# A kernel of attention and two expert layers: in the second layer, the next expert's rows are fetched ahead of the output so far

## The chip, the cores and the metric

The program runs on one core of a Trainium2 chip. The metric is the device time of one execution in microseconds (us), as the median of several runs. TensorE (PE in the rows, PEld for its weight loads), VectorE (DVE), ScalarE (ACT), GpSimd (POOL) and SyncE (SP) each run their own list of instructions in order, and wait for each other by semaphores. SP issues the transfers of weights on one DMA queue, POOL issues the indirect transfers (rows picked by a list of row numbers) on another; both queues share 16 DMA engines.

## The reference, cut to what matters

Attention makes a table of 1152 tokens with 512 numbers each. A first layer sends each token to one of 8 experts. The second layer, on its result `x`, sends each token to its two best experts and adds up what they give:

```python
out = np.zeros((N, D), dtype=np.float32)
for e in range(E):
    for k in range(2):
        mask = top2[:, k] == e
        if not mask.any():
            continue
        h = np.maximum(x[mask] @ w1[e], 0.0)
        out[mask] += top2_w[mask, k, None] * (h @ w2[e])
return out.astype(np.float32)
```

Here N is 1152, D is 512, E is 8, and the hidden width of an expert is 1024.

## The kernel before

The kernel first does the attention, then the eight experts of the first layer, then the eight of the second. Only the loop over the experts 1 to 7 of the second layer is touched (lines 1775 to 1783 before); one pass of it is called an expert here.

An expert takes up to 288 tokens in the straight path: two blocks of 128 rows, and a third block of 32 rows that is only computed if the expert has more than 256 tokens. That third block is `rest(e)`, behind a branch at line 1780. Every number is kept as a sum of two reduced-precision parts, so weights are split into a high part by ACT (line 167) and a low part by DVE (line 170) after SP has fetched them, and every product is three matmuls (lines 198 to 200).

For an expert the work is this:

- `prev` (line 1577), twice: POOL fetches the rows of the output so far for each block into `pv` (shown as `px` in rows, since these tiles were named so earlier). The output holds what the experts before have added, so this waits until the previous expert's rows have landed in memory.
- `next_rows` and `rows2` (line 1418, in `gather`): POOL fetches the rows of `x` for the next expert's two blocks into `g0` and `g1`, and for this expert's third block into `g2`. These read `x_d`, which the first layer has finished.
- `blocks`: PE makes the hidden layer (matmuls to `h`, operands `xh`, `xl`), ACT and DVE turn it into `hh` and `hl` (lines 1145 and 1148), and PE makes the output (matmuls to `y`).
- `prep`: in the midst of the `y` matmuls PE turns the fetched rows by transposes (line 1015), ACT and DVE make `xh` and `xl` of them (lines 1018 and 1021), which the next expert's first matmul reads. The third block's rows go the same way into `xp`.
- `to_out`: DVE scales `y` and adds the old rows of the output (line 1583), and POOL writes the rows back (line 1586, `out_dram<-o`).

The order on each engine is set when the program is built. `F.add` enters an operation with its engine ("P", "A", "V", "G" for PE, ACT, DVE, GpSimd), a cost and what it depends on; `F.run` is a small planner that picks, for each engine, which entry comes next; `after=` is the earliest planned time of an entry. On the chip each engine takes its list in that order whatever the planner thought of times. SP issues a load of the weight chunk that comes seven later whenever a chunk has been split.

Of the kernel before, what the change touches and what calls it, by code (L numbers as in the profile page):

```python
# [41 lines left out]
def _off(ap):  # L42
    return bass.IndirectOffsetOnAxis(ap=ap, axis=0)
# [3 lines left out]
def attention_moe_moe2(ctx, tc, q, k, v, wg1, w1a, w2a, cap, wg2, wn2, noise, w1b, w2b, out):  # L47
    nc = tc.nc
    B, H, S, D = q.shape
    E, DM, F = w1a.shape  # L50
# [67 lines left out]
    def whole(u):  # L118
        return u < 8 * E and u % 8 >= 8 - WHOLE
# [55 lines left out]
    def w1_at(e, kk, f0, f1):  # L175
        s = slot(8 * e + kk)
        return whi[s][:, f0:f1], wlo[s][:, f0:f1]
# [19 lines left out]
    def mm3(o, sh, sl, mh, ml, first, last):  # L197
        nc.tensor.matmul(o, sh, mh, start=first, stop=False)  # L198
        nc.tensor.matmul(o, sh, ml, start=False, stop=False)  # L199
        nc.tensor.matmul(o, sl, mh, start=False, stop=last)  # L200

    xT = [(wa.tile([128, KD, 256 + R], F32R, name=f"xh{i}"), wa.tile([128, KD, 256 + R], F32R, name=f"xl{i}")) for i in range(1)]
# [913 lines left out]
    def blocks(F, e, x, more, finish, deps=(), done={}, apart=False):  # L1116

        xh, xl = x
        hh, hl = hT
        hp = {}  # L1120
        lo = []
        rows = 256 + more
        per = 1 if more else 2

        def l1(f, bank=None):
            if bank is not None:
                hp[f // per] = bank
            o = hp[f // per][:, (f % per) * rows:(f % per) * rows + rows]
            for kk in range(KD):
                sh, sl = w1_at(e, kk, f * 128, f * 128 + 128)  # L1130
                mm3(o, sh, sl, xh[:, kk, :rows], xl[:, kk, :rows], kk == 0, kk == KD - 1)

        def part(t, g):
            return t[:, per * g:per * g + per, :rows]

        def of(g):
            return hp[g][:, 0:per * rows].rearrange("p (f n) -> p f n", f=per)

        def plain(g):
            w = [whole(8 * e + 4 + (per * g + i) // 2) for i in range(per)]  # L1140
            assert w[0] == w[-1]
            return w[0]

        def relu(g):
            nc.scalar.activation(part(hfull[0], g - (KF - 2 * WHOLE) // per) if plain(g) else part(hh, g), of(g), AF.Relu)  # L1145

        def low(g):
            nc.vector.scalar_tensor_tensor(part(hl, g), of(g), 0.0, part(hh, g).bitcast(F32), op0=OP.max, op1=OP.subtract)  # L1148

        p = None  # L1150
        w1 = [done.get(8 * e + kk) for kk in range(KD)]
        for g in range(KF // per):
            c = 1.62 if more else 1.44
            first = p = F.add("P", c, lambda b, g=g: l1(per * g, b), [p] + list(deps) + w1, take="h")
            for i in range(1, per):
                p = F.add("P", c, lambda g=g, i=i: l1(per * g + i), [p])
            if g == KF // per - 1:
                for kk in range(KD):
                    if 8 * e + kk in F.hold:
                        F.hold[8 * e + kk]["deps"].append(p)  # L1160
            a = F.add("A", 0.41 if more else 0.6, lambda g=g: relu(g), [p], frees=first if plain(g) else None)
            lo += [a if plain(g) else F.add("V", 0.46 if more else 0.69, lambda g=g: low(g), [a], frees=first)] * per
        a = product2(F, e, 0, finish, [p, *lo], done)
        return [a, product2(F, e, 1, finish, [ends.pop() if apart else p, *lo], done)]
# [3 lines left out]
    def product2(F, e, blk, finish, lo=None, done={}):  # L1168

        hp = {}  # L1170
        n = 128 if blk < 2 else R

        def l2(f, bank=None):
            if f == 0:
                hp["y"] = bank[:n]
            product(hp["y"], e, f, slice(blk * 128, blk * 128 + n), f == 0, f == KF - 1)

        p, *lo = lo or [None] * (KF + 1)
        for f in range(KF):
            d = [p, lo[f], done.get(8 * e + 4 + f // 2)]  # L1180
            if f == 0:
                p = first = F.add("P", takes(e, f), lambda b: l2(0, b), d, take="y")
            else:
                p = F.add("P", takes(e, f), lambda f=f: l2(f), d)
        ends[:] = [p]
        return finish(lambda: hp["y"], blk, p, first)

    def splits(F, us):

        done = {}  # L1190
        for u in us:
            a = F.add("A", 0.95, lambda u=u: split(u, 0), [done.get(order[turn[u] - RAWS - MORE])], needs=u)
            F.hold[over(u)] = a
            if u % 8 in BESIDE:
                done[u] = F.add("G", 1.9, lambda u=u: split(u, 3), [a], loads=behind(u), tail=F.par["split"])
                continue
            b = F.add("V", 0.6, lambda u=u: split(u, 1), [a])
            done[u] = F.add("V", 0.6, lambda u=u: split(u, 2), [a, b], loads=behind(u), tail=F.par["split"])
        return done
# [185 lines left out]
    def count(t, e):  # L1385
        return nc.values_load(t[0:1, e:e + 1], min_val=0, max_val=NT, skip_runtime_bounds_check_because="a count of tokens")
# [17 lines left out]
    G = {}  # L1404
# [68 lines left out]
    for e in range(E):  # L1473
        for u in range(8 * e + EARLY, 8 * e + 8) if e else ():
            load(u)
        if e + 1 == E:
            F = Flow()
# [3 lines left out]
        def beside(F, first):  # L1481
            done = splits(F, units(e))
            nxt = post(F, first, last=True)[0] if first is not None else None
            if e + 1 < E:
                for blk, n in BLK:
                    d = F.add("G", 1.04, lambda blk=blk, n=n: row1(e + 1, blk, n)) if e else None
                    prep(F, lambda blk=blk: xr[e + 1, blk], n, xT[(e + 1) % 2], 128 * blk, deps=[d], when=(WHEN0 if e == 0 else F.par["when"]) + 1.5 * blk)
            else:
                d, _ = rows2(F, (0, 0), 0, 0, tis[0])
                prep(F, lambda: G[0, 0][2], 128, xT[0], 0, deps=[d])  # L1490
            return done, nxt
# [47 lines left out]
        with cmp.Else():  # L1539
            F = Flow(SMALL if e else FIRST)  # L1540
            begin(F)
            done, nxt = beside(F, last)
# [23 lines left out]
    def apart(ins, key):  # L1566

        if own["e"] != key[0]:
            own["e"], own["ins"] = key[0], []
        for o in own["ins"]:  # L1570
            tc.declare_no_dep(ins.ins, o.ins, reason="other rows")
        own["ins"].append(ins)
# [3 lines left out]
    def prev(ti, i, n=128):  # L1576
        ins = nc.gpsimd.indirect_dma_start(out=pv[i][:n], out_offset=None, in_=out, in_offset=_off(ti[:n, 0:1]),  # L1577
                                           bounds_check=NT - 1, oob_is_err=False)

    def to_out(F, y, key, i, p, first, n=128, deps=()):  # L1580
        def go():
            o = G[key, "o"] = os_[i]
            nc.vector.scalar_tensor_tensor(o[:n], y(), G[key][0][:n], pv[i][:n], op0=OP.mult, op1=OP.add)  # L1583

        def send():
            ins = nc.gpsimd.indirect_dma_start(out=out, out_offset=_off(G[key][1][:n, 0:1]), in_=G[key, "o"][:n], in_offset=None,  # L1586
                                               bounds_check=NT - 1, oob_is_err=False)
            if key[1] != "more":
                apart(ins, key)

        a = F.add("V", 0.66, go, [p, F.outs.get(i)] + list(deps), frees=first)
        F.outs[i] = F.add("G", 1.04, send, [a])
# [9 lines left out]
    def arm(e):  # L1602
        F = Flow(SECOND)
        if e + 1 < E:
            F.add("P", 0.3, lambda: many.update(n=count(cnt2, e)), after=10.0)
        done = splits(F, units(E + e))
        next_rows(F, e)
        if e + 1 == E:
            F.add("G", 0.2, lambda: nc.gpsimd.drain(), after=6.0)  # L1609
        else:  # L1610
            d, _ = rows2(F, (e, 2), e, 2, n=R)
            prep(F, lambda: G[e, 2][2], R, pair, 0, deps=[d], when=F.par["when"] + 4)
        blocks(F, E + e, xT[e % 2], 0, lambda y, blk, p, first: to_out(F, y, (e, blk), blk, p, first), done=done, apart=e + 1 == E)
        F.close(F.run())

    def rest(e):
# [123 lines left out]
    F = Flow(KNOWN)  # L1740
    done = splits(F, units(E))
# [31 lines left out]
    state["u"] = min(NU, 8 * E + SLOTS)  # L1773
    came, later = later, ({}, {})
    for e in range(1, E):
        for blk in range(2):
            prev(G[e, blk][1], blk)
        arm(e)
        if e + 1 < E:
            with tc.If(many["n"] > 256):  # L1780
                rest(e)
        state["u"] = min(NU, 8 * (E + e) + SLOTS)
        came, later = later, ({}, {})
# [32 lines left out]
```

## Time and profile before

| | |
|---|---|
| median of 3 runs (lowest, highest) | 559.38 us (557.72, 559.82) |
| the profiled execution's own time | 557.14 us |
| its span in the trace | 555.5 us |
| PE busy | 517.0 us, 93% of the span |
| DVE, ACT, POOL busy | 378.9, 294.1, 138.4 us |

The span runs from the first to the last instruction of the trace, and the execution's own time holds 1.64 us more around it. The rest of the trace is read by stage: the shares over the whole span mix attention and both layers.

### The profile page before, as it was taken

The numbers are of one execution on the slowest core, as the hardware profiler recorded it, in microseconds if no ns is written. First come the engines' busy times: TensorE is split into PE (matmuls) and PEld (weight loads), VectorE is DVE, ScalarE is ACT, GpSimd is POOL, SyncE is SP. The second block draws the span as 40 slices with busy tenths as digits, with TensorE's granted clock in tenths as the row PEclk, the third lists the DMA queues.
The fourth block names the chain that finished last, engine by engine and source line by source line (L and its number), as shares of the span: only waits on it lengthen the run. The fifth ranks groups of instructions, "written<-read, shape, count | busy, mean of one in ns | idle before, by whom it ended". The sixth has DMA issues, their size and how long they took to land. (4 is left out here: it accounts for less than half of the span.)

```text
span 555.5 us, 10106 instructions
## 1 busy us (share of the span) xinstructions
PE 517.0 (93%) x3381; PEld 422.8 (76%) x3381; DVE 378.9 (68%) x1008; ACT 294.1 (53%) x580; POOL 138.4 (25%) x225
## 2 busy tenths in 40 slices
PE   3999999999869999999999999989999999969996
PEld 3778777878647776787976967888989886949794
DVE  7899988888548988757674678464848562917441
ACT  5888878871347687544533536252635442716130
POOL 3000000000462234405233133142513132514131
PEclk9999999999999999999999999999999999979999
DMA  6998896423458878754632442638658591545220
GB/s 136 221 240 229 220 230 188 123 77 109 137 176 290 265 240 296 232 189 138 206 133 64 170 137 71 226 125 284 221 205 280 188 327 48 187 180 165 86 66 35
DMA packets 71176, 99.17 MB, mean 179 GB/s; under 512 B 37130, under 2 KB 40586, under 8 KB 71088
## 3 DMA queue, kind: packets, MB, share of 16 engines
q1 hardware_dynamic: 63600, 83.16, 47.6%
q0 software_dynamic: 6432, 14.71, 8.4%
q8 instruction: 39, 0.64, 0.5%
q14 instruction: 49, 0.40, 0.2%
q10 hardware_dynamic: 1056, 0.26, 0.2%
HBM read 87.53 MB, written 12.25 MB: 180 GB/s over the span
## 5 line engine op out<-in xcount | busy, mean ns | idle before, releaser
L170 DVE TENSOR_TENSOR wl<-raw,wh 128x512 fp32r<-128x512 f32 x140 | 91.6, 685 | 12.0 <-ACT wh L167 11.6
L167 ACT ACTIVATE wh<-raw 128x1024 fp32r<-128x1024 f32 x70 | 71.1, 1052 | 20.1 <-PEq L1780 12.5
L170 DVE TENSOR_TENSOR both<-raw,both 128x512 fp32r<-128x512 f32 x100 | 66.0, 684 | 8.9 <-ACT both L167 8.4
L167 ACT ACTIVATE both<-raw 128x1024 fp32r<-128x1024 f32 x50 | 51.3, 1054 | 10.0 <-PEq L1780 8.3
L198 PE MATMUL h<-xh,wh 128*128 128x256 f32 (+1 forms) x184 | 52.9, 287 | 0.5
L199 PE MATMUL h<-xl,wh 128*128 128x256 f32 (+1 forms) x184 | 52.6, 286 | 0.0
L200 PE MATMUL h<-xh,wl 128*128 128x256 f32 (+1 forms) x184 | 52.5, 285 | 0.0
L1018 ACT ACTIVATE xh<-tp 128x512 fp32r<-128x512 f32 (+1 forms) x37 | 19.0, 536 | 59.0 <-PE tp L1015 57.3
L1021 DVE TENSOR_TENSOR xl<-tp,xh 128x512 fp32r<-128x512 f32 (+1 forms) x37 | 21.9, 610 | 35.3 <-ACT xh L1018 35.1
L1145 ACT ACTIVATE hh<-h 128x512 fp32r<-128x512 f32 (+1 forms) x46 | 24.1, 523 | 38.7 <-PE h L200 32.3
L1586 POOL DMA_INDIRECT out_dram<-o,T2i x16 | 18.5, 1156 | 96.9 <-DVE o L1583 94.8
L1148 DVE SCALAR_TENSOR_TENSOR hl<-h,hh 128x512 fp32r<-128x512 f32 (+1 forms) x46 | 27.5, 597 | 22.1 <-ACT hh L1145 18.0
L198 PE MATMUL h<-xh,both 128*128 128x256 f32 (+1 forms) x136 | 39.2, 288 | 2.7 <-DVE hl L1148 1.4
L199 PE MATMUL h<-xl,both 128*128 128x256 f32 (+1 forms) x136 | 39.0, 287 | 0.0
L200 PE MATMUL h<-xh,both 128*128 128x256 f32 (+1 forms) x136 | 38.8, 285 | 0.0
L198 PE MATMUL y<-wh,hh 128*128 128x512 f32 (+1 forms) x94 | 38.3, 407 | 0.0
L200 PE MATMUL y<-wh,hl 128*128 128x512 f32 (+1 forms) x94 | 37.1, 394 | 0.0
L199 PE MATMUL y<-wl,hh 128*128 128x512 f32 (+1 forms) x94 | 36.9, 393 | 0.0
L550 ACT ACTIVATE pt<-s,negmax 128x128 f32<-128x128 f32 (+3 forms) x64 | 33.4, 526 | 6.4 <-DVE negmax L537 5.1
L526 PE MATMUL s<-both 128*128 128x256 f32 (+2 forms) x128 | 33.1, 371 | 3.8 <-ACT both L468 2.5
L198 PEld LDWEIGHTS h<-xh,wh 128*128 128x128 f32 x184 | 34.7, 189 | 2.1 <-issue 1.6
L199 PEld LDWEIGHTS h<-xl,wh 128*128 128x128 f32 x184 | 34.6, 188 | 0.0
(295 smaller groups left out, 1297.9 us busy)
## 6 DMA issues: line engine op xcount, KB each, us to landing
raw<-in_moe_w_dram SPq DMA_DIRECT2D x120, 512.0 KB, 5.1
wf<-in_moe_w_dram SPq DMA_DIRECT2D x8, 512.0 KB, 5.8
out_dram<-zero SPq DMA_DIRECT2D x3, 768.0 KB, 5.5
both<-both SPq DMA_DIRECT2D x14, 160.0 KB, 2.6
raw<-in_q_dram SPq DMA_DIRECT2D x16, 128.0 KB, 4.2
vn<-in_v_dram SPq DMA_DIRECT2D x16, 128.0 KB, 2.6
both<-both SPq DMA_DIRECT2D x14, 144.0 KB, 3.3
raw<-in_k_dram SPq DMA_DIRECT2D x14, 128.0 KB, 4.7
```

Source lines behind the costliest of these rows:

```text
L167: nc.scalar.activation(h, t, AF.Copy)
L170: (nc.gpsimd if part == 3 else nc.vector).tensor_sub(l[:, c], t[:, c], h[:, c].bitcast(F32))
L198: nc.tensor.matmul(o, sh, mh, start=first, stop=False)
L199: nc.tensor.matmul(o, sh, ml, start=False, stop=False)
L200: nc.tensor.matmul(o, sl, mh, start=False, stop=last)
L526: nc.tensor.matmul(o, w[:, i, h, 128 * t:128 * t + 128], w[:, i + 2, h, 64 * h:64 * h + n], start=(i == 0), stop=(i == 1))
L550: nc.scalar.activation(o, i, AF.Exp, bias=negmax[:, pr, 2 * t + h:2 * t + h + 1], accum_out=ssum[b][:, t, 2 * p + h:2 * p + h + 1])
L1018: nc.scalar.activation(xh[:, :, c0:c0 + n], h["tp"][:, :, :n], AF.Copy)
L1021: nc.vector.tensor_tensor(xl[:, :, c0:c0 + n], h["tp"][:, :, :n], xh[:, :, c0:c0 + n].bitcast(F32), op=OP.subtract)
L1145: nc.scalar.activation(part(hfull[0], g - (KF - 2 * WHOLE) // per) if plain(g) else part(hh, g), of(g), AF.Relu)
L1148: nc.vector.scalar_tensor_tensor(part(hl, g), of(g), 0.0, part(hh, g).bitcast(F32), op0=OP.max, op1=OP.subtract)
L1586: ins = nc.gpsimd.indirect_dma_start(out=out, out_offset=_off(G[key][1][:n, 0:1]), in_=G[key, "o"][:n], in_offset=None, bounds_check=NT - ...
```

## The change

The two calls of `prev` at the head of the loop's body are taken out. They become two planned entries inside `arm`, behind the entries for the fetches of the next expert's rows, with an earliest planned time of 3.5 (0 for the last expert), and the DVE operation that adds the old rows depends on them.

```diff
@@ def arm(e), e from 1 to 7
         else:
             d, _ = rows2(F, (e, 2), e, 2, n=R)
             prep(F, lambda: G[e, 2][2], R, pair, 0, deps=[d], when=F.par["when"] + 4)
-        blocks(F, E + e, xT[e % 2], 0, lambda y, blk, p, first: to_out(F, y, (e, blk), blk, p, first), done=done, apart=e + 1 == E)
+        before_ = [F.add("G", 1.04, lambda blk=blk: prev(G[e, blk][1], blk), after=3.5 if e + 1 < E else 0.0) for blk in range(2)]
+        blocks(F, E + e, xT[e % 2], 0, lambda y, blk, p, first: to_out(F, y, (e, blk), blk, p, first, deps=[before_[blk]]), done=done, apart=e + 1 == E)
         F.close(F.run())
...
     for e in range(1, E):
-        for blk in range(2):
-            prev(G[e, blk][1], blk)
         arm(e)
```

POOL's list at the head of an expert, as the planner makes it, with the difference between before and after (`g` with a number is a tile for fetched rows of `x`, `px` one for rows of the output):

```order
-L1577 DMA px_1732<-out_dram,T2i 128x512
-L1577 DMA px_1733<-out_dram,T2i 128x512
 L1418 DMA g_1740<-x_d,T2i 128x524
 L1418 DMA g_1741<-x_d,T2i 128x524
 L1418 DMA g_1742<-x_d,T2i 32x524
+L1577 DMA px_1732<-out_dram,T2i 128x512
+L1577 DMA px_1733<-out_dram,T2i 128x512
 L1386 TENSOR_LOAD cnt_92
 L1586 DMA out_dram<-o_6630,T2i 1152x512
 L1586 DMA out_dram<-o_6631,T2i 1152x512
```

The three fetches of `x` rows now stand ahead of the two fetches of the output, in experts 1 to 6 alike; in expert 7, which has no next expert, POOL's list is as it was. The lists of PE, DVE, ACT and SP are the same before and after, but for the numbers of source lines.

## Rows read from the trace of the kernel before

**Rows 1.** The page's head, and its slices of the granted TensorE clock.

```profile
span 555.5 us, 10106 instructions
...
PEclk9999999999999999999999999999999999979999
```

**Rows 2.** Busy by stretch, experts 3, 5: PE PEld DVE ACT POOL, clock, DMA.

```profile
412.40:436.70 24.30, 24.15 (x158) 21.37 (x157) 15.59 (x25) 11.35 (x15) 7.26 (x7) 1.00 0.67 235
474.00:501.40 27.40, 22.44 (x129) 19.11 (x129) 13.34 (x23) 9.37 (x14) 9.55 (x6) 0.88 0.54 186
```

**Rows 3.** Waits of PE from 366 to 556 us: total, times, longest.

```profile
PE tp L1015 <- DMA g<-x_d,T2i: 5.0, 2, 4.6
PE h L198 <- DVE hl L1148: 1.4, 1, 1.4
```

**Rows 4.** PE in time order, expert 5: start, us, what, idle before.

```profile
488.03 0.39 PE L200 MATMUL y<-both,hl 128*128 128x512 f32 x1
493.06 1.12 PE L1015 MATMUL tp<-ident,g 128*128 128x128 f32 x4 [4.64 <-DMA g<-x_d,T2i]
494.49 1.11 PE L1015 MATMUL tp<-ident,g 128*128 128x128 f32 x4 [0.32 <-DMA g<-x_d,T2i]
...
498.86 0.40 PE L199 MATMUL y<-both,hh 128*128 128x512 f32 x1
```

**Rows 5.** The same place of PE's list in expert 3.

```profile
430.83 0.39 PE L200 MATMUL y<-wh,hl 128*128 128x512 f32 x1
431.06 1.03 PE L1015 MATMUL tp<-ident,g 128*128 128x128 f32 x8
...
434.12 0.39 PE L199 MATMUL y<-wl,hh 128*128 128x512 f32 x1
```

**Rows 6.** Stretches around that wait; last columns: clock, DMA share, GB/s.

```profile
488.00:490.00 2.00, 0.42 (x2) 0.00 (x0) 0.00 (x0) 0.00 (x0) 0.94 (x1) 1.00 0.94 359
490.00:492.00 2.00, 0.00 (x0) 0.00 (x0) 0.00 (x0) 0.00 (x0) 0.00 (x0) 0.86 1.03 419
492.00:493.00 1.00, 0.00 (x0) 0.00 (x0) 0.00 (x0) 0.00 (x0) 0.00 (x0) 0.50 0.80 316
...
494.00:495.00 1.00, 0.68 (x4) 0.51 (x4) 0.16 (x1) 0.60 (x1) 0.00 (x0) 0.50 0.01 4
```

**Rows 7.** POOL in order of time, head of expert 5.

```profile
473.91 2.92 POOL L1586 DMA_INDIRECT out_dram<-o,T2i  x1 [5.11 <-DVE o L1583]
481.15 1.84 POOL L1577 DMA_INDIRECT px<-out_dram,T2i  x1 [4.31 <-DMA out_dram<-o,T2i]
483.29 1.47 POOL L1577 DMA_INDIRECT px<-out_dram,T2i  x1 [0.30 <-issue]
485.08 1.46 POOL L1418 DMA_INDIRECT g<-x_d,T2i  x1 [0.32 <-issue]
486.84 1.00 POOL L1418 DMA_INDIRECT g<-x_d,T2i  x1 [0.30 <-issue]
488.15 0.94 POOL L1418 DMA_INDIRECT g<-x_d,T2i  x1 [0.30 <-issue]
```

**Rows 8.** POOL in order of time, head of expert 3.

```profile
415.70 1.08 POOL L1586 DMA_INDIRECT out_dram<-o,T2i  x1 [0.31 <-issue]
419.02 1.11 POOL L1577 DMA_INDIRECT px<-out_dram,T2i  x1 [2.24 <-DMA out_dram<-o,T2i]
...
423.17 1.00 POOL L1418 DMA_INDIRECT g<-x_d,T2i  x1 [0.30 <-issue]
```

**Rows 9.** DVE in order of time, end of expert 5.

```profile
502.32 1.43 DVE L1583 SCALAR_TENSOR_TENSOR o<-y,T,px 128x512 f32<-128x512 f32 x2 [3.09 <-PE y L200]
```

**Rows 10.** Expert 3: SP's first weight loads, ACT's last split and last `hh`.

```profile
416.60 7.72 SPq L159 DMA_DIRECT2D raw<-in_moe_w_dram  x4
...
422.47 1.05 ACT L167 ACTIVATE wh<-raw 128x1024 fp32r<-128x1024 f32 x1
...
426.33 0.60 ACT L1145 ACTIVATE hh<-h 128x512 fp32r<-128x512 f32 x1 [2.32 <-PE h L200]
```

## The prediction

> **What bounds the kernel now.** I read the page's head first. The profiled execution spans 555.5 us; PE is busy for 93% of it, and the granted clock is at its upper level in every slice of the page but one, which shows a 7 [rows 1]. PE is the bound, so only what makes PE idle or slow in the second layer can pay. That one slice, the 36th of 40, lies at 486 to 500 us, and points to a place.
>
> The table by stretch is next. Expert 3 shows the usual state: PE is busy 24.15 of 24.30 us at clock 1.00. Expert 5 has 22.44 of 27.40 us busy, at a mean clock of 0.88 [rows 2]. The list of PE's waits says what for: in all of the experts 1 to 7 the transposes at line 1015 wait twice for fetched rows of `x`, 5.0 us in total and 4.6 us at the longest; the next entry is 1.4 us [rows 3]. In order of time both waits turn out to lie in expert 5, where the last `y` matmul before the transposes starts at 488.03 and the transposes at 493.06 and 494.49 [rows 4]. The other five experts that transpose show no such wait; expert 3 stands for them [rows 5].
>
> The idle time is not the whole price. The granted clock is 1.00 to 490 us, averages 0.86 in the next two, and is 0.50 (the 1.2 GHz level) from 492 [rows 6], after PE had stood idle. So four transposes take 1.12 us, where eight take 1.03 us in expert 3 [rows 4, 5].
>
> Why expert 5: POOL's list. Expert 4 had more than 256 tokens, so its third block was computed and its rows written back, at 473.91 for 2.92 us. The first `prev` waits for that write to land and starts at 481.15. The three fetches of `x`, which need nothing of the output, stand behind both `prev`, at 485.08, 486.84 and 488.15 [rows 7]. PE wants the first at about 488.4, 3.4 us after its issue. In expert 3 the write needs no third block, the `prev` start at 419.02, and the second fetch of `x` is issued at 423.17, 7.9 us before the transposes [rows 5, 8].
>
> **What it removes, and its size.** The same piece of PE's list, from the last `y` matmul before the transposes to the second one behind all three of them, takes 434.12 - 430.83 = 3.29 us in expert 3 and 498.86 - 488.03 = 10.83 us in expert 5 [rows 4, 5]. The difference, 7.54 us, is idle time and slow clock together. It comes back whole if all three fetches land before PE wants them.
>
> **When they would land.** POOL is free behind the third block's write at 473.91 + 2.92 = 476.83; with the usual 0.30 between issues the first fetch starts at 477.13, 8.0 us earlier than now [rows 7]. Nothing else holds it: `x` is final, and the tiles `g` were last read by expert 4's transposes. Its time to land is no row of its own. Expert 5 bounds it from above, since transposes that wait start when the rows are there: 493.06 - 485.08 = 7.98 us for the first, 494.49 - 486.84 = 7.65 us for the second [rows 4, 7]. A lower bound is not needed, since earlier is as good. I take 8.0 us, though the DMA engines are less full then. The issues themselves I take at the slowest pace of the five in expert 5, 1.84 us [rows 7], so the fetches start at 477.13, 479.27 and 481.41, and land by 485.1, 487.3 and 489.4. PE wants the first two from 488.4, one after the other, and the third behind eight transposes and six matmuls, some 2.4 us later (434.12 - 431.06 = 3.06 less the four small transposes and the next matmul [rows 5]). So all are in time, the second by 1.1 us or more and the third by about 1.4. At 2.92 us an issue, the slowest POOL row there [rows 7], the second would start at 480.35 and land by 488.4: still in time, just. Fetches at 0.94 us, the fastest, only add room.
>
> Issues that meet a busy DVE took 1.46 to 1.84 us, those that met an idle one 0.94 to 1.00 [rows 7] (the stretches from 488 have DVE idle [rows 6]). The Trainium skill, "SBUF — State Buffer", section "Who interferes with whom", says that a DVE instruction with two inputs in SBUF contends with a GpSimd instruction that reads SBUF, and that the later one blocks. The change moves three issues into a stretch where DVE is splitting weights, so the rule speaks against it; the trace agrees in direction, and the slow pace above is what it costs here.
>
> **What is moved.** The two `prev` fall behind three fetches. In expert 5 they would start at 481.41 + 1.84 + 0.30 = 483.6 and 485.7, 2.4 us later than now, and land by 493.7 at the same 8.0 us. DVE wants them at 502.32 now [rows 9], at 494.8 once 7.54 us are gone: hidden by about 1 us. Should they be late, DVE's add and the write wait, but PE's next matmuls go to `h` and not to `y`, so PE pays only once `y` is wanted again, more than 10 us later. In expert 3, a `prev` at 419.02 becomes one at about 415.70 + 1.08 + 0.30 + 3 x 1.4 = 421.3 [rows 8], with more than 12 us to DVE's add. Cost nothing; the cover is the whole of PE's `y` stage. Expert 7 has the same list as before, and so has the first layer.
>
> In experts 1 to 4 and 6 the fetches start some 4 to 5 us earlier too, but PE did not wait for them there, so nothing comes of it. The weights that the next expert needs are not late after expert 5 is shortened: the DMA engines are done at 494 (share 0.01 from 494 to 495 [rows 6]), and the next expert would start at 503.1 - 7.5 = 495.6.
>
> **The sum.** 557.14 - 7.54 = 549.6 us for the profiled execution's own time. The median of the runs, 559.38, is 2.24 us above it; I take the difference as it is: 559.38 - 7.54 = 551.84, about 551.8 us, 1.3% less.
>
> **The rivals.** Half a per cent, 2.8 us, is about what a measurement of this kernel can tell from no change.
>
> *No change: the rows land with the weights.* The wait ended at 493.06, just as the DMA engines ran dry: their share falls from 1.03 to 0.80 to 0.01 [rows 6]. If row fetches were served only as the weight loads end, an earlier issue would gain nothing: 559.4 us. Against it: in expert 3 the mean DMA share is 0.67 over the whole stretch, with loads in flight, and rows issued at 423.17 were there by 431 [rows 2, 5, 8]; and the third block's write landed before 481.15, in the midst of expert 5's loads [rows 7]. I give it 7%. The Trainium skill, "DMA: Bandwidth & Descriptors", section "Anatomy of one DMA — SWDGE (gpsimd) path", fits such a DMA as 2.0 us plus its bytes at 436 GB/s; for 128 rows of 524 floats that is an estimate of 2.6 us. By that page the rows issued at 485.08 would have been there at 487.7, PE would never have waited, and the change would give nothing; the trace has 7.98 us and a wait, and decides.
>
> *Half: under full load a landing takes longer than 8 us.* If the rows come 1 to 3 us late, PE idles that long, perhaps without the slow clock: 553 to 556 us. Speaks for it: only two landings bound my 8.0. 6%.
>
> *Slower: the weights of the split in hand come late.* SP's first load of an expert, issued at 416.60 in expert 3, is split in the same expert, by ACT at 422.47, and ACT's last `hh` stands behind that split with 2.32 us of idle time before it [rows 10]. Fetches moved ahead take DMA time from that load. It costs PE time from the point where the load is late by more than 2.3 us; the moved bytes are two fetches of 268 KB, which at 300 GB/s (the rate that rows 6 and 2 lie around) is 1.8 us, so it should not be reached. If it were late by 4.5 us in all six experts, 6 x 2.2 = 13 us would come back: 559.4 - 7.5 + 13.2 = 565 us. 4%.
>
> **How the numbers follow.** All three fetches in time: 83%, 551.8 us, give or take 1.5 us by the spread of the runs before. With half (6%), no change (7%) and slower (4%), faster by over half a per cent is 0.88 (half included up to 556.6), no change 0.08, slower 0.04. The low end, 549.0, takes the case that the 2.24 us between median and profile is more of the same wait in the other runs; the high end, 555.5, reaches into the half case. That leaves out no change and slower.
>
> **What would show it.** In the profile after: no wait of the transposes at line 1015 for `x_d` in expert 5; the first fetch of that expert right behind the third block's write, before that has landed; the granted clock at 1.00 through that stage and no 7 in its slices; expert 5 as long as the others; `prev` some 2 us later in each expert, with no wait of DVE's add for it. The prediction is wrong if PE still waits there, if ACT waits for raw weights, or if POOL does not issue the fetches until the write has landed.

## The result and the profile after

| | before | after |
|---|---|---|
| median (lowest, highest), 4 runs each on one chip | 558.55 us (555.88, 559.82) | 549.48 us (548.57, 553.26) |
| the profiled execution's own time | 557.14 us | 548.57 us |
| its span | 555.5 us | 546.9 us |

The ratio of after to before is 0.9871, with a 95% interval of 0.984 to 0.9903: faster by 1.3%.

The page of the changed kernel, its head and the slices of the granted clock, which answer to [rows 1]:

```profile
span 546.9 us, 10105 instructions
...
PEclk9999999999999999999999999999999999999999
```

The one low slice is gone. The table by stretch, for experts 3 and 5, answers to [rows 2]; behind the five engines stand clock, DMA share and GB/s. The two stretches are now alike, PE busy for all but 0.15 us of each.

```profile
412.80:437.00 24.20, 24.05 (x158) 21.34 (x156) 15.53 (x26) 11.34 (x15) 7.56 (x7) 1.00 0.69 235
470.30:494.60 24.30, 24.15 (x159) 21.40 (x157) 15.82 (x27) 11.74 (x17) 12.42 (x6) 1.00 0.61 209
```

PE's waits from 364 us to the end, all of them, in place of [rows 3]: the transposes at line 1015 no longer appear, and the longest entry is the one of 1.2 us that stood second before.

```profile
PE h L198 <- DVE hl L1148: 1.2, 1, 1.2
PE y L1657 <- DVE hh L1636: 0.3, 1, 0.3
PE h L198 <- PEq L1779: 0.2, 1, 0.2
```

PE in order of time in expert 5, the same place as [rows 4]: from the last `y` matmul before the transposes to the second one behind them it is 490.37 - 487.08 = 3.29 us, where it was 10.83, and the eight transposes take 1.03 us again.

```profile
487.08 0.39 PE L200 MATMUL y<-both,hl 128*128 128x512 f32 x1
487.31 1.03 PE L1015 MATMUL tp<-ident,g 128*128 128x128 f32 x8
...
489.68 0.43 PE L1015 MATMUL tp<-ident,g 32*128 32x32 f32 x4
...
490.37 0.39 PE L199 MATMUL y<-both,hh 128*128 128x512 f32 x1
```

POOL in order of time at the head of expert 5, in place of [rows 7] (the first row is the third block's write, then three fetches of `x` and the two of the output):

```profile
473.04 2.92 POOL L1586 DMA_INDIRECT out_dram<-o,T2i  x1 [5.09 <-DVE o L1583]
476.27 2.23 POOL L1418 DMA_INDIRECT g<-x_d,T2i  x1 [0.30 <-issue]
478.81 3.27 POOL L1418 DMA_INDIRECT g<-x_d,T2i  x1 [0.30 <-issue]
482.38 1.41 POOL L1418 DMA_INDIRECT g<-x_d,T2i  x1 [0.30 <-issue]
484.10 1.59 POOL L1577 DMA_INDIRECT px<-out_dram,T2i  x1 [0.30 <-issue]
485.99 0.99 POOL L1577 DMA_INDIRECT px<-out_dram,T2i  x1 [0.30 <-issue]
```

The first fetch starts 0.30 us behind the write, without waiting for it to land. The fetches themselves take up to 3.27 us to issue, longer than any fetch of this layer did before (1.84 us). The write starts 0.87 us earlier than before; counted from it, the output's rows are asked for 3.6 to 3.8 us later than they were. DVE's add of this expert waits for `y` alone:

```profile
493.81 1.43 DVE L1583 SCALAR_TENSOR_TENSOR o<-y,T,px 128x512 f32<-128x512 f32 x2 [3.06 <-PE y L200]
```

The span is 8.6 us shorter, of which expert 5 gives 7.5 and 0.4 lie elsewhere in the layer. Another 0.68 us lies ahead of anything that the change touches: expert 1's first matmul starts that much earlier. First the row of before, then the row of after:

```profile
363.97 0.35 PE L198 MATMUL h<-xh,both 128*128 128x256 f32 x1 [0.30 <-PEq L1771]
```

```profile
363.29 0.35 PE L198 MATMUL h<-xh,both 128*128 128x256 f32 x1 [0.30 <-PEq L1772]
```

### The profile page after: what moved, and what is told of

The parts are those of the page before. It is cut to its first block, busy times and chain, and to the rows that moved or that the text cites. A ratio compares the mean times of both kernels' runs of the same rounds, so it can differ in the third digit from the quotient of the medians.

```text
span 546.9 us, 10105 instructions
## 1 busy us (share of the span) xinstructions
PE 514.3 (94%) x3381; PEld 421.5 (77%) x3381; DVE 378.8 (69%) x1008; ACT 293.9 (54%) x580; POOL 139.7 (26%) x225
## 5 line engine op out<-in xcount | busy, mean ns | idle before, releaser
L1437 POOL MEMSET xr<- 128x524 f32 x3 | 1.5, 547 | 131.5 <-DVE T1f L811 131.5
```

## The experiments

The theory is that of the prediction: the gain is one wait in expert 5, idle time and slow clock together, and it exists only because the fetches stood behind a `prev` that waited for the third block's write. The rivals are a gain spread over the experts, rows that land only when the weight loads end, and a place among the weight loads, instead of the third block's write, as the cause. Ratios are to the kernel before, run beside each experiment.

**Expert 5 alone, and every expert but 5.** The new order is taken under a condition, `e == 5` in the first kernel and `e != 5` in the second; the other experts keep the two fetches of the output at the head. Against the changed kernel, for the first of the two:

```diff
-        before_ = [F.add("G", 1.04, lambda blk=blk: prev(G[e, blk][1], blk), after=3.5 if e + 1 < E else 0.0) for blk in range(2)]
+        ahead = e == 5
+        before_ = [F.add("G", 1.04, lambda blk=blk: prev(G[e, blk][1], blk), after=3.5 if e + 1 < E else 0.0) if ahead else None for blk in range(2)]
...
     for e in range(1, E):
+        for blk in range(2):
+            if not (e == 5):
+                prev(G[e, blk][1], blk)
         arm(e)
```

> The change in expert 5 alone; in the other experts the two fetches of the output stand first, as before. Theory: the whole gain is expert 5's wait, 10.83 - 3.29 = 7.5 us, so the time is that of the changed kernel, about 549.5 to 551 us (ratio 0.987), and no transposes at line 1015 wait. Rival, the gain is spread over the six experts (shorter heads of POOL's list, less contention): a sixth of it, about 557 us (ratio 0.998).

> The change in every expert but 5. Theory: nothing is gained, ratio 1.00 (558.6 us), and the transposes of expert 5 wait about 5 us as before. Rival, the gain is spread over the experts: five sixths of it, about 552 us (ratio 0.989).

Expert 5 alone: 550.54 us against 557.81, ratio 0.9879 (0.9848 to 0.9909), no wait at line 1015. Every expert but 5: 557.71 us, ratio 0.9992 (0.9965 to 1.002), and the wait is there as before. The whole gain is expert 5's, and a gain spread over the experts falls. The wait of the second kernel, from the list of PE's waits and from PE in order of time:

```profile
PE tp L1015 <- DMA g<-x_d,T2i: 4.8, 1, 4.8
```

```profile
488.40 0.39 PE L200 MATMUL y<-both,hl 128*128 128x512 f32 x1
493.57 2.07 PE L1015 MATMUL tp<-ident,g 128*128 128x128 f32 x8 [4.78 <-DMA g<-x_d,T2i]
```

**PE kept busy through the wait.** The order of before, with matmuls that do no useful work ahead of expert 5's first transposes, in the bank that these then write.

```diff
...
+            for _ in range(20 if fill else 0):
+                nc.tensor.matmul(bank, hT[0][:, 0, 0:128], whi[slot(fill)][:, 0:512], start=True, stop=True)
             for kk in range(KD):
...
```

> The order of before, with 20 matmuls of 128x512 put on PE ahead of expert 5's first transposes (about 0.23 us each, 4.6 us, into the bank that the transposes then overwrite). They do no useful work. Theory: PE idles there for 4.96 us in any case, so they cost nothing, and the granted clock stays at 1.00, so the part of the 7.54 us that is slow clock, 7.54 - 4.96 = 2.6 us, comes back: about 556 us (ratio 0.995). Rival, the transposes and matmuls behind the wait are slow for another reason than the clock (the rows only trickle in): no gain, ratio 1.00 or a little above.

555.08 us, ratio 0.9956 (0.9934 to 0.9977): 2.7 us faster than before with 20 matmuls more. PE in order of time, and below it the stretches of the same time, ending in clock, DMA share and GB/s:

```profile
487.87 0.40 PE L200 MATMUL y<-both,hl 128*128 128x512 f32 x1
488.11 4.81 PE L1010 MATMUL tp<-both,hh 128*128 128x512 f32 x20
492.76 0.64 PE L1017 MATMUL tp<-ident,g 128*128 128x128 f32 x4
494.20 0.66 PE L1017 MATMUL tp<-ident,g 128*128 128x128 f32 x4 [0.80 <-DMA g<-x_d,T2i]
...
496.88 0.39 PE L199 MATMUL y<-both,hh 128*128 128x512 f32 x1
```

```profile
488.00:492.00 4.00, 4.00 (x19) 3.25 (x18) 0.00 (x0) 0.00 (x0) 0.91 (x1) 1.00 1.00 386
492.00:494.00 2.00, 1.40 (x8) 0.82 (x7) 0.00 (x0) 0.56 (x1) 0.00 (x0) 1.00 0.47 187
```

The rows still land no earlier (the second four transposes wait for them until 494.20, close to where they start in [rows 4]), but the clock stays at 1.00 and four transposes take 0.64 us, where they took 1.12. This piece takes 496.88 - 487.87 = 9.01 us, 1.8 us less than the 10.83 of before; the medians say 2.7, with an interval of 1.3 to 3.7. So some 2 to 3 of the 7.5 us were the slow clock behind the idle time, and the rest was the idle time.

**One of the three fetches ahead.** The order of before, but in expert 5 the first fetch of `x` stands ahead of the two fetches of the output, the other two behind them.

```diff
+        def go():
+            if key == (6, 1):
+                for j in range(2):
+                    prev(G[5, j][1], j)
+            gather(F, key, gs[blk if i is None else i], n)
...
-            prev(G[e, blk][1], blk)
+            if e != 5:
+                prev(G[e, blk][1], blk)
```

> The order of before, but in expert 5 the first of the three row fetches is put ahead of the two fetches of the output; the second and third stay behind them. Theory (a landing takes up to 8 us from its issue): the first is issued at about 477 us and is in time, the second at about 485 us and lands at 492 to 493, PE idles about 3.5 us behind its first four transposes, and the gain is 1 to 4 us of the 7.5 (ratio 0.993 to 0.998). Rival (rows land only when the weight loads end): the first four transposes wait as before too, ratio 1.00, idle time of 4.6 us ahead of the first. Rival (one fetch is enough): the whole gain, ratio 0.987.

555.52 us, ratio 0.9968 (0.9941 to 0.9995), a gain of 2.3 us by the medians. POOL and PE in order of time, then two stretches:

```profile
477.26 2.24 POOL L1424 DMA_INDIRECT g<-x_d,T2i  x1 [0.31 <-issue]
...
485.16 1.50 POOL L1424 DMA_INDIRECT g<-x_d,T2i  x1 [0.30 <-issue]
```

```profile
488.40 0.60 PE L1015 MATMUL tp<-ident,g 128*128 128x128 f32 x4
492.61 0.66 PE L1015 MATMUL tp<-ident,g 128*128 128x128 f32 x4 [3.60 <-DMA g<-x_d,T2i]
```

```profile
490.00:492.00 2.00, 0.00 (x0) 0.00 (x0) 0.36 (x1) 0.00 (x0) 0.00 (x0) 1.00 1.04 419
...
494.00:495.00 1.00, 1.00 (x3) 0.33 (x1) 0.62 (x1) 0.00 (x0) 0.00 (x0) 0.50 0.00 0
```

The first fetch was in time, though the DMA engines were busy until after 492 us, so rows do land in the midst of weight loads, and that rival falls. The second, at its old place behind the two fetches of the output, landed 492.61 - 485.16 = 7.45 us after its issue and made PE idle for 3.60 us. Each fetch is late or not by its own place in the list. The clock was still 1.00 while PE stood idle here and when it took up work again, and was 0.50 from 494 us.

**Without the third block.** The branch at line 1780 is set to more than 1100 rows, so that no third block is computed and expert 4's rows beyond 256 are left out, once with the order of before and once with the changed order.

```diff
-            with tc.If(many["n"] > 256):
+            with tc.If(many["n"] > 1100):
                 rest(e)
```

> The order of before, with the branch to the third block set to more than 1100 rows instead of 256, so that no third block is computed and expert 4's rows beyond 256 are left out. Theory: what delays the fetches in expert 5 is the landing of the third block's write, so without it expert 5's wait is gone: 8.97 us of the third block and 7.5 us of the wait less, about 541.5 us (ratio 0.971), clock 1.00 throughout. Rival, expert 5 waits for another reason (its place among the weight loads): only the third block's 9 us go, about 549 us (ratio 0.984).

> The changed kernel, likewise without the third block (the same rows left out). Theory: behind a straight expert the order of the fetches gives nothing, so the time is that of the order of before without the third block, within 0.3%: about 541 us (ratio 0.970). Rival, the order gives something in every expert: 3 us or more below it.

541.46 us with the order of before (ratio 0.9723, 0.9686 to 0.976), 541.51 us with the changed order (ratio 0.9715, 0.9681 to 0.9749): the same. The forecast of 1.00 for the clock held in expert 5 but not for the whole: the profiled execution has a mean of 0.993, with low stretches in the first layer (see the last section). With the order of before the fetch that PE waited for most follows the write by 470.67 - 464.01 = 6.7 us now, where it was 485.08 - 473.91 = 11.2 us in [rows 7], and the transposes wait for nothing. POOL, then PE, of that kernel:

```profile
464.01 1.05 POOL L1586 DMA_INDIRECT out_dram<-o,T2i  x1 [0.30 <-issue]
467.92 1.12 POOL L1577 DMA_INDIRECT px<-out_dram,T2i  x1 [2.86 <-DMA out_dram<-o,T2i]
...
470.67 1.14 POOL L1418 DMA_INDIRECT g<-x_d,T2i  x1 [0.30 <-issue]
```

```profile
479.43 1.03 PE L1015 MATMUL tp<-ident,g 128*128 128x128 f32 x8
```

Expert 5 keeps its place among the weight loads there, and does not wait; the third block is the cause, and without it the order of the fetches is worth nothing that these runs show. Of the 4.5 us by which the fetch follows sooner, 3.3 lie between the start of the write and the first `prev` (3.91 us, where it was 7.24), and 1.2 in the two `prev`, which are issued faster. These kernels leave out the whole third block, so no run tells the landing of its write from the slower issues behind it.

**Fetched an expert earlier.** All fetches of `x` are issued in the expert before, once PE's transposes have read the tile; the two fetches of the output stand alone at the head.

```diff
...
+                t = prep(F, lambda blk=blk: G[e + 1, blk][2], n, xT[(e + 1) % 2], 128 * blk, deps=[d], when=F.par["when"] + 2 * blk)
+                if e + 2 < E:
+                    rows2(F, (e + 2, blk), e + 2, blk, n=n, deps=[t])
...
```

> Every fetch of rows of x is issued an expert earlier, as soon as PE's transposes have read the tile it goes to (some 17 to 20 us into the expert before); the two fetches of the output stand alone at the head, as in before. Theory: PE's wait in expert 5 is gone and nothing else was waited for, so the time is that of the changed kernel, 549 to 551 us (ratio 0.987), with no wait at line 1015 and a spread no wider. Rival, the fetches also crowd the weight loads at the head of each expert: 2 us or more below the changed kernel.

> The changed kernel once more, beside the others on one chip: 549 to 551 us (ratio 0.987), no wait of the transposes at line 1015.

Early: ratio 0.9858 (0.9823 to 0.9893), its median 551.12 us; one of its executions took 1719.51 us, which nothing here explains, and the comparison leaves it out. The changed kernel beside it: 550.64 us, ratio 0.9884 (0.9852 to 0.9916). The two can't be told apart; neither waits at line 1015. Taking the fetches off the head of the experts altogether gives nothing beyond what the change gave. No version here beats the changed kernel clearly.

## Why the prediction was right

- **Where the gain is.** One wait, in expert 5, and only there: the change in that expert alone gives the whole of it, and in all others none of it.
- **Its size.** 7.54 us by the two pieces of PE's list; 10.83 us became 3.29 us, as in expert 3. By ratio the forecast was 551.84 / 559.38 = 0.9865, the measured one 0.9871. In absolute terms the median came out 2.4 us lower than forecast, at 549.48: 0.8 us because the median of before fell to 558.55 with its fourth run, 1.5 us because these medians differ by 9.1 us and not by 7.54. The medians of the repeats differ by 7.3 us (expert 5 alone) and 6.6 us (the changed kernel again), and the interval of the ratio, 0.984 to 0.9903, or 5.4 to 8.9 us, holds these and 7.54, but not 9.1. So 9.1 us does not speak for a second gain, and how close the median came to the low end of the range, 549.0, is chance as far as these runs show.
- **The split of idle time and clock.** Filling the wait kept the clock at 1.00 and gave back 2.7 us by the medians and 1.8 us by the piece of PE's list, around the 2.6 us that follow from 7.54 less the waits of [rows 4].
- **When the rows land.** The time of 8.0 us from issue, taken from the two waits, held as an upper bound where it could be seen again: 7.45 us in the kernel with one fetch ahead. The issues were mis-sized: the fetches took 2.23, 3.27 and 1.41 us, where I had 1.84 as the slow pace and 2.92 as the bound. Counted from the third block's write, the second fetch started 5.77 us behind it (forecast 5.36) and the third 9.34 us (forecast 7.50). For the first two the cover was enough. The third would by 8.0 us have landed at 490.38, 0.7 us after its transposes at 489.68; they did not wait, so its 32 rows landed within 7.3 us. That this fetch was in time was luck by the prediction's own terms.
- **What was moved.** The fetches of the output start 11.06 and 12.95 us behind the write (forecast 9.7 and 11.8). The second would by 8.0 us have landed at 493.99, and DVE's add starts at 493.81 without a wait for it: the cover of about 1 us was used up, and the rows came sooner than the bound.
- **The rivals.** No change and the half case fall with the kernels above. The slower one, weight loads that come late, does not show: no wait of ACT for raw weights, and the kernel with the change in every expert but 5 has ratio 0.9992.
- **The low end of the range** rested on a reading that no run shows: that the 2.24 us between the profile and the median of before were more of the same wait. The time also varies in another place, the first layer (below). How much of it the wait had in the runs without a profile stays open.
- **What slows the issues.** The prediction laid the slow issues to a busy DVE, from expert 5 alone. The fetch of [rows 8] at 423.17 took 1.00 us in the midst of DVE's weight splits:

```profile
421.31 2.58 DVE L170 TENSOR_TENSOR both<-raw,both 128x512 fp32r<-128x512 f32 x4
423.82 0.68 DVE L170 TENSOR_TENSOR wl<-raw,wh 128x512 fp32r<-128x512 f32 x1
```

So a busy DVE does not slow every issue, and the reading that the trace agrees does not hold beyond expert 5. What slowed the issues there stays open; the prediction took the slow pace from rows, whatever its cause.

## What to carry to other kernels

In a queue that issues in order, look for a transfer that waits, and at what stands behind it without needing that wait; put the ones that need nothing first, and count the wait against the moment when the slowest consumer wants them. Such an order is worth only what the late stage is worth: here the one expert behind a third block paid, and the five others with the new order did not, so read the price from that stage and not from a share of the whole. An idle TensorE can cost twice: here the wait of 5 us, and some 2 to 3 us of slow clock behind it.

## What the runs showed of the hardware that was not expected

The same instructions in the same place lose the clock in one execution and not in another. The stretches from 154 to 160 us, where the first layer waits for rows, of the kernel with the order of before and no third block, and then of the changed kernel's second profile (PE, PEld, DVE, ACT, POOL, clock, DMA share, GB/s); up to there the two have the same instructions:

```profile
154.00:156.00 2.00, 0.81 (x5) 0.81 (x6) 0.19 (x1) 0.00 (x0) 1.65 (x5) 0.89 1.07 325
156.00:158.00 2.00, 1.70 (x4) 0.78 (x3) 0.69 (x1) 0.60 (x1) 1.72 (x7) 0.50 0.88 322
158.00:160.00 2.00, 1.75 (x8) 1.41 (x8) 0.10 (x1) 0.60 (x1) 1.40 (x2) 0.75 0.42 159
```

```profile
154.00:156.00 2.00, 1.44 (x8) 1.07 (x8) 0.12 (x1) 0.60 (x1) 1.95 (x6) 1.00 1.04 393
156.00:158.00 2.00, 0.63 (x6) 0.52 (x6) 0.57 (x1) 0.00 (x0) 1.43 (x6) 1.00 0.87 317
158.00:160.00 2.00, 2.00 (x11) 1.12 (x10) 0.69 (x1) 0.74 (x2) 0.94 (x1) 1.00 0.06 8
```

PE was busy for 4.26 of these 6 us in the first and 4.07 in the second, but only the first fell to 0.50 (1.2 GHz). In the profile of the kernel before it was busy for 2.80 of them, and the clock stayed at 1.00. So the idle time of this stretch alone does not tell which execution loses the clock. The times of the changed kernel go with its mean clock: 548.57 us at 1.000, 549.38 at 0.999, 549.58 at 0.998, 553.26 at 0.993, a spread of 4.7 us without any change of the program. The clock is not the whole of such a spread: at a mean clock of 0.988 the kernel before took 555.93 us in one execution and 558.46 in another.

An indirect fetch of `x` took 0.92 to 1.02 us to issue in the kernel that fetches an expert earlier, where it waits for PE's transposes, and 1.41 to 3.27 us in expert 5 of the changed kernel, amid DVE's weight splits, though 1.00 us amid splits in expert 3 of the kernel before. The long one is no accident of one execution: 3.28 us in the same place in the profiles of expert 5 alone and of the changed kernel run again. What makes it long was not tried.
